# W0 as one transfer on the ScalarE queue, and one filler group fewer before the first transposes

## The chip, the core and the metric

The kernel runs on one core of a Trainium2 chip. The metric is device time in microseconds (us) of one execution. Most numbers below are medians of 3 to 11 executions; a trace is one execution. An execution is called slow when it took over 1.5% longer than the fastest of the same kernel in the same set, and fast otherwise; the ratios below use fast executions alone. Most matmuls of this kernel are printed by the timeline with a tile of 128*32, and the program issues them in sets of four on four such tiles; such a set is called a group. In the traces the four run side by side: in the trace before, a group of 512 columns takes about 0.22 us, less than the 0.38 us (median) that one of its matmuls lasts. The clock record of the trace before has two values, 1.0 and 0.5. I call them full and half clock, and half clock also the time before the first entry, where such a group takes 0.43 us in the trace after.

## The reference, cut to what matters

```python
# x0: 4096 x 416, ws: 6 x 416 x 416, bs: 6 x 416, all bf16
x = x0
for l in range(6):
    x = x0 * (x @ ws[l] + bs[l]) + x
return x
```

The kernel keeps x transposed (features on partitions). The 416 features are three chunks of 128 and a tail of 32. Rows go in four blocks of 1024. A layer of a block is 4.87 us of nearly gapless TensorE work, 24 times.

## The kernel before: the start-up

Only the start-up is touched. Of the first block, three pieces of 256 rows are loaded as they are and transposed on TensorE; its last 256 rows and the other blocks come by transposing transfers. W0, the weights of the first layer, comes in two transfers: its first third (`k == 0`) as the third load of SyncE, the other two thirds as the second load of ScalarE.

```python
# SyncE
sp.dma_start(bsa_sb[1:L + 1, :], bs[:, :]).then_inc(s_bs, 16)
sp.dma_start(xin_sb[:, 0:2, :], x0_v[:, 0:2, :]).then_inc(s_xin[0], 16)   # "x load 0"
sp.dma_start(w_sb[:, 0, 0, :], ws[0, 0:128, :]).then_inc(s_w0, 16)
sp.dma_start(xin_sb[:, 4:6, :], x0_v[:, 4:6, :]).then_inc(s_xin[2], 16)
sp.dma_start_transpose(x0T_sb[:, :, 768:SB], x0[768:SB, 0:DF]).then_inc(s_x0T[0], 16)
# ... cut: W1 to W5 and the other blocks of x
# ScalarE
act.dma_start(xin_sb[:, 2:4, :], x0_v[:, 2:4, :]).then_inc(s_xin[1], 16)  # "x load 1"
act.dma_start(w_sb[:, 0, 1:NC, :], ...).then_inc(s_w[0], 16)
act.dma_start(xtl_sb[:, :, :], x0_v[:, 6:JS, DF:D]).then_inc(s_xtl0, 16)  # "x tail load"
# ... cut
# TensorE
def fill(n):              # matmuls of constants whose result nobody reads
    for i in range(n):
        for q in range(4):
            tile_mm(ps[lane(q), 7, 0:256], const[:, 0:32], const, q, True)
fill(10)
bias_sums()
fill(2)
pe.wait_ge(s_set, 1)
for i, (h, c) in enumerate(IN_ORDER):      # six transposes of x load 1, then six of x load 0
    if c == 0:
        pe.wait_ge(s_xin[h], 16)
    # ... cut: two transposes into PSUM, then s_inT
# layer 0 of block 0
pe.wait_ge(s_w0, 16)
for k in range(NC):
    if k == 1:
        pe.wait_ge(s_w[0], 16)
    if k == 2:
        pe.wait_ge(s_xin[2], 16); pe.wait_ge(s_xtl0, 16)
        tail_inputs(); third_input()
    before_a(k)           # k == 0: waits for three VectorE copies of transposed x
    for m in range(NC):
        # ... cut
        step(m, 0, k)
```

The filler is meant to keep TensorE busy until the loads land. After this part TensorE goes on to the tail matmuls (those that read the 32-feature tail), and from there everything is periodic.

Of the kernel before, what the change touches and what calls it, by code (L numbers as in the profile page):

```python
# [11 lines left out]
def bass_standalone__dcn_v2_cross__recsys_kernel(  # L12
# [8 lines left out]
    NC = 3  # L21
    DF = 128 * NC
# [10 lines left out]
    with ExitStack() as es:  # L33
        block = es.enter_context(nc.Block())

        def sb(name, shape, dt=BF16):
            return es.enter_context(nc.sbuf_tensor(name, shape, dt))

        w_sb = sb("w_sb", [128, L, NC, D])
# [23 lines left out]
        def sem(name):  # L63
            return es.enter_context(nc.semaphore(name))

        s_ones, s_set, s_w0, s_zero = sem("s_ones"), sem("s_set"), sem("s_wk0"), sem("s_zero")
        s_wtp, s_wc = sem("s_wtp"), [sem("s_wc%d" % i) for i in range(2)]
        s_bs, s_cbp, s_cb = sem("s_bs"), sem("s_cbp"), sem("s_cb")
        s_xin = [sem("s_xin%d" % i) for i in range(3)]
# [1 line left out]
        s_w = [sem("s_w%d" % i) for i in range(L)]  # L71
# [15 lines left out]
        def wmain(l):  # L87
            return ws[l, 0:DF, :].rearrange("(k p) n -> p k n", p=128)
# [10 lines left out]
        def lane(g):  # L99
            return slice(32 * g, 32 * g + 32)  # L100
# [4 lines left out]
        def load_wt(eng, g, a, b, done):  # L105
            n0, n1 = ((0, 256), (256, DF))[g % 2]
            eng.dma_start(
                wt_sb[lane(g), a:b, 0:n1 - n0], ws[a:b, DF:D, n0:n1].rearrange("l p n -> p l n")
            ).then_inc(done, 16)

        @block.sync
        def _(sp):
            def load_rows(s):
                sp.dma_start_transpose(
                    x4_sb[:, s - 1:s, :], x0[s * SB:(s + 1) * SB, D - 128:D]
                ).then_inc(s_x4[s - 1], 16)
                sp.dma_start_transpose(
                    x0T_sb[:, :, s * SB:(s + 1) * SB], x0[s * SB:(s + 1) * SB, 0:DF]
                ).then_inc(s_x0T[s], 16)

            sp.dma_start(bsa_sb[1:L + 1, :], bs[:, :]).then_inc(s_bs, 16)  # L121
            sp.dma_start(xin_sb[:, 0:2, :], x0_v[:, 0:2, :]).then_inc(s_xin[0], 16)  # L122
            sp.dma_start(w_sb[:, 0, 0, :], ws[0, 0:128, :]).then_inc(s_w0, 16)
            sp.dma_start(xin_sb[:, 4:6, :], x0_v[:, 4:6, :]).then_inc(s_xin[2], 16)
            sp.dma_start_transpose(x0T_sb[:, :, 768:SB], x0[768:SB, 0:DF]).then_inc(s_x0T[0], 16)
            for l in range(1, L):
                if l > 1:
                    sp.wait_ge(s_ti, (1, 2, 2, 2)[l - 2])
                if l == L - 1:
                    load_rows(1)  # L130
                sp.dma_start(w_sb[:, l, :, :], wmain(l)).then_inc(s_w[l], 16)
                if l == 1:
                    for g in range(4):
                        load_wt(sp, g, 1, L, s_wt[1])
            for s in range(NS - 1):
                n = (s + 1) * L
                sp.wait_ge(s_xa, NC * n)
                sp.wait_ge(s_xb, NC * n)
                for c in range(NC):
                    sp.dma_start_transpose(  # L140
                        o_sb[:, s * JS:(s + 1) * JS, c * 128:(c + 1) * 128], xo_sb[:, s, c, :]
                    ).then_inc(s_oT, 16)
                sp.wait_ge(s_xt, n)
                sp.dma_start_transpose(ot_sb[:, s, :, :], xot_sb[:, s, :]).then_inc(s_ot, 16)
                if s < NS - 2:
                    load_rows(s + 2)
                sp.wait_ge(s_oT, 16 * NC * (s + 1))
                sp.wait_ge(s_otc, s + 1)
                sp.dma_start(
                    out_v[:, s * JS:(s + 1) * JS, :], o_sb[:, s * JS:(s + 1) * JS, :]  # L150
                ).then_inc(s_out, 16)
            j = (NS - 1) * JS
            sp.wait_ge(s_oeA, 2)
            sp.dma_start(out_v[:, j:j + 4, 0:256], o_sb[:, j:j + 4, 0:256]).then_inc(s_out, 16)
            sp.wait_ge(s_oeA, 3)
            sp.wait_ge(s_oet, 1)
            sp.dma_start(out_v[:, j:j + 4, 256:D], o_sb[:, j:j + 4, 256:D]).then_inc(s_out, 16)
            sp.wait_ge(s_oeD, 2)
            sp.wait_ge(s_oet, 1)
            sp.dma_start(out_v[:, j + 6:j + 8, :], o_sb[:, j + 6:j + 8, :]).then_inc(s_out, 16)  # L160
            sp.wait_ge(s_out, 16 * (NS + 3))
# [48 lines left out]
        def _(pe):  # L210
            def tile_mm(dst, lhsT, rhs, q, start):
                return pe.matmul(  # L212
                    dst, lhsT=lhsT, rhs=rhs, start=start, stop=True,
                    skip_group_check=True, tile_position=(0, 32 * q),
                )
# [3 lines left out]
            def fill(n):  # L219
# [4 lines that stand above are left out]
            def tail_inputs():  # L224
                for r in range(2):
                    for g in range(4):
                        for i in range(2):
                            j = 2 * (g ^ i) + r
                            src = xin_sb[:, j, DF:D] if j < 6 else xtl_sb[:, j - 6, :]
                            ins = tile_mm(ps[lane(g), 5, i * G + r * 128:i * G + r * 128 + 128], src, ident[:, :], g, True)  # L230
                ins.then_inc(s_tp, 1)

            def third_input():
                pe.wait_ge(s_inD, 4)
                for c in range(NC):
                    for j in range(2):
                        for q in range(4):
                            f0 = c * 128 + 32 * q
                            ins = tile_mm(
                                ps[lane(q), THIRD[c], j * 128:j * 128 + 128], xin_sb[:, 4 + j, f0:f0 + 32], ident[:, :], q, True  # L240
                            )
                    ins.then_inc(s_inT, 1)

            def bias_sums():
                pe.wait_ge(s_bs, 16)
                pe.wait_ge(s_zero, 2)
                pe.wait_ge(s_set, 2)
                for c in range(NC + 1):
                    for q in range(4):
                        f0 = c * 128 + 32 * q if c < NC else DF  # L250
                        ins = tile_mm(ps[lane(q), 1, c * 8:c * 8 + L], bsa_sb[:, f0:f0 + 32], u_sb[:, :], q, True)
                ins.then_inc(s_cbp, 1)

            fill(10)
            bias_sums()
            fill(2)
            pe.wait_ge(s_set, 1)
            for i, (h, c) in enumerate(IN_ORDER):
                if c == 0:
# [17 lines left out]
            for s in range(NS):  # L277
                for l in range(L):
                    n = s * L + l
# [25 lines left out]
                    def before_a(k):  # L305
                        if n == 0:
                            pe.wait_ge((s_inD, s_inA, s_inD)[k], (3, 2, 4)[k])
                        else:
                            pe.wait_ge(s_xa, NC * (n - 1) + k + 1)
                            if l == 0 and k == 0:  # L310
                                pe.wait_ge(s_x0T[s], 16)

                    if n == 0:
                        pe.wait_ge(s_w0, 16)
                        for k in range(NC):
                            if k == 1:
                                pe.wait_ge(s_w[0], 16)
                            if k == 2:
                                pe.wait_ge(s_xin[2], 16)
                                pe.wait_ge(s_xtl0, 16)  # L320
                                tail_inputs()
                                third_input()
                            before_a(k)
                            for m in range(NC):
                                if k == 0 and m == 1:
                                    pe.wait_ge(s_cb, 1)
                                step(m, 0, k)
                    else:
                        if s == 0:
                            pe.wait_ge(s_w[l], 16)  # L330
                        chunk(0, 0, before_a)
                        chunk(1, 0)
                        chunk(2, 0)
# [140 lines left out]
        @block.scalar  # L474
        def _(act):
            act.dma_start(xin_sb[:, 2:4, :], x0_v[:, 2:4, :]).then_inc(s_xin[1], 16)
            act.dma_start(w_sb[:, 0, 1:NC, :], ws[0, 128:DF, :].rearrange("(k p) n -> p k n", p=128)).then_inc(s_w[0], 16)
            act.dma_start(xtl_sb[:, :, :], x0_v[:, 6:JS, DF:D]).then_inc(s_xtl0, 16)
            for g in (1, 3):
                load_wt(act, g, 0, 1, s_wt[0])  # L480
# [15 lines left out]
            for s in range(NS):  # L496
                for l in range(L):
                    n = s * L + l + 1
# [75 lines left out]
```

## Time and profile before

| | before |
|---|---|
| median, first 3 executions (range) | 131.13 us (130.83 to 131.14) |
| span of the profiled execution | 128.6 us |
| layer 0 starts | 5.46 us |
| tail matmuls start | 8.15 us |

Three lines of the page of the kernel before: TensorE's busy time with its share of the span, then the chain of work that ended last, by engine and by line.

```profile
PE 124.0 (96%) x2440; PEld 62.3 (48%) x2440; DVE 100.1 (78%) x154; ACT 71.4 (56%) x163; POOL 22.5 (18%) x41
PE 92%; DMA 3%; DVE 1%; SPq 1%; issue 0%; DVEq 0%
PE ps L212 82%; PE ps L353 10%; DMA w_sb<-in_ws_dram 3%; DVE xo_sb L461 1%; DVE o_sb L466 0%; SPq L122 0%; SPq L121 0%; DVEq L33 0%; PE ps L369 0%
```

So TensorE is the bound, and the only load in the chain is W0. The chain of the first 9 us, in order of time (start, duration, what; SPq is SyncE's queue):

```profile
0.81 0.39 SPq L121
1.26 0.42 SPq L122
1.73 3.68 DMA w_sb<-in_ws_dram
5.41 0.04 issue
5.46 2.76 PE ps L212 x75
8.22 0.32 PE ps L353
```

In this execution layer 0 starts because the first third of W0 lands at 5.41 us, and from there TensorE is never released by a load again. The timeline of the same kernel (start, duration, engine, line, operation, count, and the idle time before it in brackets) shows the rest of the start-up:

```profile
3.30 0.62 PE L212 MATMUL ps<-const-bfloat16-1.0 128*32 128x256 bf16 x8
3.85 1.46 PE L262 MATMUL ps<-ident,xin_sb 128*128 128x128 bf16 x12
4.28 1.36 DVE L438 COPY x0T_sb<-ps 128x256 bf16<-128x256 bf16 x4 [0.65 <-PE ps L262]
5.46 1.55 PE L212 MATMUL ps<-x0T_sb,w_sb 128*32 128x512 bf16 x24
5.76 0.75 PEld L212 LDWEIGHTS ps<-x0T_sb,w_sb 128*32 128x32 bf16 x16 [0.17 <-issue]
8.15 0.39 PE L353 MATMUL ps<-x0t_sb,wt_sb 32*128 32x512 bf16 x1
```

The twelve transposes run without a break, and the 24 first matmuls of layer 0, six groups of 512 columns, take 1.55 us: about 0.22 us a group after the first. A filler group of only 256 columns takes 0.21 us, so the array then runs at half the rate. The page's PEclk row prints full clock in every slice and does not show this; the clock record in the trace file does: its first entry is full clock, and it begins at 5.66 us. (The half clock before the first entry is not in the mean granted clock of an execution either: this one's mean is 1.000.)

### The profile page before, as it was taken

What the parts mean: (1) busy time and instruction counts of PE and PEld (TensorE: products, weight loads), DVE (VectorE), ACT (ScalarE), POOL (GpSimd) and SP (SyncE); (2) the same over time, 40 slices, a digit from 0 to 9 for tenths busy, and PEclk for the clock granted to TensorE, in tenths of its full rate; (3) what the DMA queues carried; (4) which work ended last, traced back from release to release, by engine and by line L of the source; (5) the groups of instructions that cost most, each with busy time, mean ns of one, the idle gap of its engine ahead of it and who ended that gap; (6) DMA issues with size and microseconds to landing.
All of it is one profiled execution on the core that took longest, in us unless ns stands there. A gap on an engine that the chain in (4) does not pass through costs nothing.

```text
span 128.6 us, 5388 instructions
## 1 busy us (share of the span) xinstructions
PE 124.0 (96%) x2440; PEld 62.3 (48%) x2440; DVE 100.1 (78%) x154; ACT 71.4 (56%) x163; POOL 22.5 (18%) x41
## 2 busy tenths in 40 slices
PE   7999999999999999999999999999999999999980
PEld 5564544545444444444444445445445445445450
DVE  2349779779779779779779779779779779789780
ACT  0637357377737357377736456476745555555670
POOL 7502202202202103102102113012012013022130
PEclk9999999999999999999999999999999999999999
DMA  3974399500009689700009686800009800800026
GB/s 102 293 175 105 90 230 167 148 0 5 3 11 140 128 130 211 255 0 5 5 0 180 117 158 146 270 0 0 5 0 85 190 0 0 270 0 5 3 79 191
DMA packets 32898, 12.54 MB, mean 98 GB/s; under 512 B 25318, under 2 KB 32876, under 8 KB 32876
## 3 DMA queue, kind: packets, MB, share of 16 engines
q1 hardware_dynamic: 31500, 11.48, 43.2%
q10 hardware_dynamic: 1184, 0.67, 1.9%
q8 instruction: 19, 0.31, 1.0%
q0 software_dynamic: 192, 0.06, 0.2%
q14 instruction: 3, 0.02, 0.1%
HBM read 2.90 MB, written 3.41 MB: 49 GB/s over the span
## 4 chain that ended last, share of the span: by engine, by line
PE 92%; DMA 3%; DVE 1%; SPq 1%; issue 0%; DVEq 0%
PE ps L212 82%; PE ps L353 10%; DMA w_sb<-in_ws_dram 3%; DVE xo_sb L461 1%; DVE o_sb L466 0%; SPq L122 0%; SPq L121 0%; DVEq L33 0%; PE ps L369 0%
## 5 line engine op out<-in xcount | busy, mean ns | idle before, releaser
L461 DVE SCALAR_TENSOR_TENSOR xT_sb<-ps,cb_sb,x0T_sb 128x512 bf16<-128x512 f32 x120 | 80.9, 743 | 16.4 <-PE ps L353 16.4
L212 PE MATMUL ps<-xT_sb,w_sb 128*32 128x512 bf16 (+1 forms) x1680 | 89.0, 364 | 0.0
L212 PEld LDWEIGHTS ps<-xT_sb,w_sb 128*32 128x32 bf16 x1680 | 43.1, 97 | 38.6 <-issue 4.2
L488 ACT ACTIVATE xt_sb<-xt_sb 32x256 bf16<-32x256 bf16 x80 | 33.1, 414 | 16.6 <-POOL xt_sb L199 15.9
L508 ACT ACTIVATE t_sb<-ps,cb_sb 64x256 f32<-64x256 f32 x48 | 22.5, 468 | 30.1 <-PE ps L212 29.8
L199 POOL TENSOR_TENSOR xt_sb<-t_sb,x0t_sb 128x256 bf16<-128x256 f32 x20 | 13.4, 672 | 84.1 <-ACT t_sb L508 84.1
L212 PE MATMUL ps<-x0T_sb,w_sb 128*32 128x512 bf16 (+1 forms) x336 | 18.5, 365 | 0.1
L461 DVE SCALAR_TENSOR_TENSOR xo_sb<-ps,cb_sb,x0T_sb 128x512 bf16<-128x512 f32 x23 | 15.6, 744 | 3.7 <-PE ps L353 3.3
L212 PEld LDWEIGHTS ps<-x0T_sb,w_sb 128*32 128x32 bf16 x336 | 8.5, 97 | 7.9 <-issue 1.0
L353 PE MATMUL ps<-xt_sb,wt_sb 32*128 32x512 bf16 x80 | 12.2, 380 | 0.0
L521 ACT ACTIVATE x0t_sb<-x_sb 32x256 bf16<-32x256 bf16 x24 | 9.9, 413 | 0.4
L369 PE MATMUL ps<-xt_sb,wt_sb 32*128 32x512 bf16 x40 | 7.8, 386 | 0.0
L353 PE MATMUL ps<-xt_sb,wc_sb 32*128 32x256 bf16 x80 | 7.7, 268 | 0.0
L353 PEld LDWEIGHTS ps<-xt_sb,wt_sb 32*128 32x128 bf16 x80 | 2.3, 93 | 8.5 <-DVE xT_sb L461 8.5
L353 PEld LDWEIGHTS ps<-xt_sb,wc_sb 32*128 32x128 bf16 x80 | 4.0, 94 | 2.3
L199 POOL TENSOR_TENSOR xot_sb<-t_sb,x0t_sb 128x256 bf16<-128x256 f32 x4 | 2.7, 671 | 12.6 <-ACT t_sb L508 12.6
L212 PE MATMUL ps<-const-bfloat16-1.0 128*32 128x256 bf16 x48 | 2.9, 414 | 0.8 <-PEq L559 0.8
L483 ACT ACT_TABLE_LOAD x1 | 1.3, 1283 | 3.3 <-issue 3.3
L353 PE MATMUL ps<-x0t_sb,wt_sb 32*128 32x512 bf16 x16 | 2.4, 380 | 0.0
L212 PEld LDWEIGHTS ps<-const-bfloat16-1.0 128*32 128x32 bf16 x48 | 1.7, 133 | 1.1 <-issue 0.8
L168 POOL DMA_DIRECT2D wc_sb<-in_ws_dram x4 | 2.2, 550 | 0.0
L443 DVE CAST x0T_sb<-ps 128x256 bf16<-128x256 f32 x2 | 0.8, 420 | 1.8 <-PE ps L212 1.8
(43 smaller groups left out, 28.8 us busy)
## 6 DMA issues: line engine op xcount, KB each, us to landing
out_dram<-o_sb SPq DMA_DIRECT2D x3, 832.0 KB, 4.1
w_sb<-in_ws_dram SPq DMA_DIRECT2D x5, 312.0 KB, 4.3
xin_sb<-in_x_dram SPq DMA_DIRECT2D x2, 208.0 KB, 3.5
out_dram<-o_sb SPq DMA_DIRECT2D x1, 256.0 KB, 2.4
xin_sb<-in_x_dram ACTq DMA_DIRECT2D x1, 208.0 KB, 2.7
w_sb<-in_ws_dram ACTq DMA_DIRECT2D x1, 208.0 KB, 3.4
out_dram<-o_sb SPq DMA_DIRECT2D x1, 208.0 KB, 2.2
out_dram<-o_sb ACTq DMA_DIRECT2D x1, 208.0 KB, 2.7
```

Of the source, the lines that this page charges most:

```text
L168: pool.dma_start(wc_sb[lane(g), a:b, 32 * g:32 * g + 32], ws[a:b, DF:D, DF:D].rearrange("l p n -> p l n")).then_inc(s_wc[i], 16)
L199: pool.tensor_tensor(out=dst, in0=t32_sb[:, n % 2, :], in1=x0t_sb[:, s, 0:G], op=ALU.mult).then_inc(s_xt, 1)
L212: return pe.matmul(dst, lhsT=lhsT, rhs=rhs, start=start, stop=True, skip_group_check=True, tile_position=(0, 32 * q),)
L353: return pe.matmul(dst, lhsT=lhsT, rhs=srct[lane(g), cols], start=l == 0 and start, stop=True, skip_group_check=True, tile_position=(32 * ...
L369: pe.matmul(ps[:, NC * h + 2, :], lhsT=wt_sb[lane(g), l, 0:128], rhs=srct[lane(g), :].rearrange("p (b r) -> p b r", b=2)[:, ::-1, :], star ...
L443: dve.tensor_copy(out=x0T_sb[:, c, 512:768], in_=ps[:, THIRD[c], 0:G]).then_inc(s_inD, 1)
L461: dve.scalar_tensor_tensor(out=dst, in0=ps[:, NC * half + c, :], scalar=cb_sb[:, c, l:l + 1], in1=x0T_sb[:, c, o:o + H], op0=ALU.add, op1= ...
L483: act.activation(out=x0T_sb[:, 1, h * 256:(h + 1) * 256], in_=psT[:, IN_BANKS[h][1], 0:256], func=ACTF.Copy).then_inc(s_inA, 1)
L488: ins = act.activation(out=buf[lane(g), G:2 * G], in_=buf[lane(g ^ 1), 0:G], func=ACTF.Copy)
L508: ins = act.activation(out=t32_sb[HALVES[h], n % 2, :], in_=tail(h), func=ACTF.Identity, bias=cb_sb[HALVES[h], NC, l:l + 1],)
L521: ins = act.activation(out=x0t_sb[lane(g), s + 1, swap * G:(swap + 1) * G], in_=x4_sb[96:128, s, r * G:(r + 1) * G], func=ACTF.Copy,)
```

## The change

The intent: the first layer should not wait for a third load of SyncE when ScalarE's second load brings the rest of the same matrix earlier; and with an earlier start, less filler is needed.

```diff
-            sp.dma_start(w_sb[:, 0, 0, :], ws[0, 0:128, :]).then_inc(s_w0, 16)
...
             fill(10)
             bias_sums()
-            fill(2)
+            fill(1)
...
-                        pe.wait_ge(s_w0, 16)
+                        pe.wait_ge(s_w[0], 16)
                         for k in range(NC):
-                            if k == 1:
-                                pe.wait_ge(s_w[0], 16)
...
-            act.dma_start(w_sb[:, 0, 1:NC, :], ...).then_inc(s_w[0], 16)
+            act.dma_start(w_sb[:, 0, :, :], wmain(0)).then_inc(s_w[0], 16)
```

Cut: the semaphore `s_w0` is no longer made.

More of the change, by code (lines that the diff above doesn't have):

```diff
@@ L64, in sem @@
             return es.enter_context(nc.semaphore(name))
-        s_ones, s_set, s_w0, s_zero = sem("s_ones"), sem("s_set"), sem("s_wk0"), sem("s_zero")
+        s_ones, s_set, s_zero = sem("s_ones"), sem("s_set"), sem("s_zero")
         s_wtp, s_wc = sem("s_wtp"), [sem("s_wc%d" % i) for i in range(2)]
@@ L476, in _ @@
             act.dma_start(xin_sb[:, 2:4, :], x0_v[:, 2:4, :]).then_inc(s_xin[1], 16)
-            act.dma_start(w_sb[:, 0, 1:NC, :], ws[0, 128:DF, :].rearrange("(k p) n -> p k n", p=128)).then_inc(s_w[0], 16)
+            act.dma_start(w_sb[:, 0, :, :], wmain(0)).then_inc(s_w[0], 16)
             act.dma_start(xtl_sb[:, :, :], x0_v[:, 6:JS, DF:D]).then_inc(s_xtl0, 16)
```

## The prediction

> **What bounds the kernel.** TensorE. The page gives PE 124.0 us of a 128.6 us span (96%), and the chain of work that ended last is 92% PE, 3% "DMA w_sb". Every later layer takes 4.87 us, which the change doesn't touch. Only the first 8.7 us can move.
>
> **The start-up before (timeline, chain, transfers).** Filler, bias sums, 8 fillers from 3.30 to 3.92 us, 12 transposes from 3.85, layer 0 from 5.46. The chain there reads: SyncE issues 0.81 and 1.26, then the first third of W0 from its issue at 1.73 for 3.68 us, so it lands at 5.41. The other two thirds (ScalarE queue, issued 1.27, 3.4 us) land at 4.65. Layer 0 also needs the third VectorE copy of the transposed x, which ends at 5.21: a limit only 0.2 us behind.
>
> **What the change does.**
> - The first third of W0 moves from SyncE's third place to ScalarE's second: one transfer of 312 KB, where there were 208 KB. The 208 KB had sent their packets by about 4.25 us; the extra 104 KB are 128 packets of 832 bytes, 0.32 us at the observed 40 packets per 100 ns, twice that if shared with SyncE's next load. My estimate for the landing of all of W0 is 5.15 us (4.95 to 5.45). [...]
> - SyncE drops one issue (0.45 us): the third x load (lands 6.35) and the transposed x load (7.92) come up to 0.5 us earlier. Neither ends a wait now. The x tail load on ScalarE gets later, from 5.84 to about 6.2, still in time.
> - One filler group (4 matmuls, 0.21 us a group) goes. The first transposes can start at about 3.64, as x of the first two blocks landed at 3.49. The second half waits for a load that landed at 4.23; its transposes began at 4.46. So the third copy ends near 5.04.
>
> **On the path.** Layer 0 should start at about 5.22, 0.24 us earlier. That isn't kept whole: before 5.66 us the clock is half. The trace's clock record gives full clock only from 5.66 us on; a filler group of 256 columns takes 0.21 us, as does a group of 512 columns later. [...] Work done before 5.66 counts half, so the gain is about 0.12 us.  The wait at 8.05 is for copies of the third x block, which move with TensorE itself.
>
> **Predicted: 131.0 us**, range 130.5 to 131.5; faster by over 2%: 0.01, within 2%: 0.98, slower by over 2%: 0.01.
>
> **What would show it.** W0 as one transfer landing between 4.95 and 5.45 us; first transpose near 3.64; first layer-0 matmul near 5.2; full clock from about 5.66; first tail matmuls about 0.1 us before 8.15; 4.87 us per layer unchanged.
>
> **What would make it wrong.** (a) W0 lands after 5.41: then no gain, or a loss of some tenths, again halved by the cold clock. [...] (c) The later tail load or tail weights end a wait at 6.6 or 8.0.

It came to this: layer 0 starts at 5.22 us instead of 5.46, 0.24 us earlier; work before 5.66 us counts half, so 0.12 us are left, and 131.13 us (the median before) less 0.12 us is 131.0 us. The landing of W0, 5.15 us, was an estimate from the trace before: it lies between 4.65 + 0.32 = 4.97 us and 4.65 + 0.64 = 5.29 us, the second if another load shares the time. That loads share it the trace does show: from 3.5 to 4.0 us one of the two hardware queues moved 171 packets and the other 50, and from 3.2 to 3.5 us 29 and 101, at 341 and 355 GB/s in all.

## The result, and the profile after

| | before | after |
|---|---|---|
| median of 6 executions (range) | 131.05 us (130.78 to 131.22) | 130.74 us (130.29 to 132.34) |
| ratio of the fast executions | 1 | 0.9969, 95% interval 0.9946 to 0.9992 |
| profiled execution | 130.45 us, fast | 132.34 us, slow |

A ratio here is the mean time of one kernel's fast runs over the mean of the other's fast runs of the same rounds, so it is not quite the ratio of the medians. The ratio leaves out the slow execution; with it the means are 130.94 us after and 131.01 us before. One of the six executions after is 1.1 us longer than any other of the two kernels in this table (132.34 against 131.22), and it is the one that was profiled. I use its trace to see what a slow execution is, not for the size of the gain.

The chain of the kernel after (line numbers have moved by 1 to 3):

```profile
0.81 0.39 SPq L121
1.27 3.33 DMA xin_sb<-in_x_dram
4.61 0.05 issue
4.65 0.82 PE ps L261 x6
5.47 0.05 issue
5.52 4.51 PE ps L211 x76
10.04 0.32 PE ps L350
```

W0 has left the chain: as one transfer it landed at 5.11 us. In its place stands x load 0, which landed at 4.61 us here against 4.23 us in the trace before, with the same issue and nothing in its own queue changed ahead of it. And the matmuls that took 2.76 us from the start of layer 0 to the tail matmuls now take 4.51 us. The timeline of the kernel after says why:

```profile
3.31 0.40 PE L211 MATMUL ps<-const-bfloat16-1.0 128*32 128x256 bf16 x4
3.73 1.74 PE L261 MATMUL ps<-ident,xin_sb 128*128 128x128 bf16 x12
4.65 0.55 PEld L261 LDWEIGHTS ps<-ident,xin_sb 128*128 128x128 bf16 x6 [0.39 <-DMA xin_sb<-in_x_dram]
5.52 2.75 PE L211 MATMUL ps<-x0T_sb,w_sb 128*32 128x512 bf16 x24
5.90 0.18 PEld L211 LDWEIGHTS ps<-x0T_sb,w_sb 128*32 128x32 bf16 x4 [0.25 <-issue]
6.33 0.18 PEld L211 LDWEIGHTS ps<-x0T_sb,w_sb 128*32 128x32 bf16 x4 [0.25 <-issue]
6.75 0.18 PEld L211 LDWEIGHTS ps<-x0T_sb,w_sb 128*32 128x32 bf16 x4 [0.25 <-issue]
9.97 0.38 PE L350 MATMUL ps<-x0t_sb,wt_sb 32*128 32x512 bf16 x1
```

The weight loads come 0.42 to 0.43 us apart: a group of 512 columns takes twice its time of before. The clock record agrees: full clock from 9.31 us, not from 5.66 us. The transposes are now broken in two by the wait for x load 0. After the start-up nothing differs: from the start of the tail matmuls to the end of the span it is 128.6 - 8.15 = 120.5 us before and 130.5 - 9.97 = 120.5 us after.

So two questions are open. Does the change itself make the clock late, or can that happen to the kernel before too? And is the gain of 0.3 us of the fast executions a gain of the change?

### The profile page after: what moved, and what is told of

Same layout as the page of the kernel before. It is cut to its first block, busy times and chain, and to the rows that moved or that the text cites. A ratio compares the mean times of both kernels' runs of the same rounds, so it can differ in the third digit from the quotient of the medians.

```text
span 130.5 us, 5378 instructions
## 1 busy us (share of the span) xinstructions
PE 125.8 (96%) x2436; PEld 62.9 (48%) x2436; DVE 100.3 (77%) x154; ACT 71.5 (55%) x163; POOL 22.6 (17%) x41
## 3 DMA queue, kind: packets, MB, share of 16 engines
HBM read 2.90 MB, written 3.41 MB: 48 GB/s over the span
## 4 chain that ended last, share of the span: by engine, by line
PE 93%; DMA 3%; DVE 1%; SPq 0%; issue 0%; DVEq 0%
PE ps L211 82%; PE ps L350 10%; DMA xin_sb<-in_x_dram 3%; PE ps L261 1%; DVE xo_sb L458 1%; DVE o_sb L463 0%; SPq L121 0%; DVEq L33 0%; PE ps L366 0%
## 5 line engine op out<-in xcount | busy, mean ns | idle before, releaser
L211 PE MATMUL ps<-x0T_sb,w_sb 128*32 128x512 bf16 (+1 forms) x336 | 19.8, 383 | 0.0
L489 ACT ACTIVATE x0t_sb<-ps 128x512 bf16<-128x512 f32 x1 | 0.6, 597 | 3.1 <-PE ps L211 3.1
```

The lines of the kernel that those rows point to most:

```text
L211: return pe.matmul(dst, lhsT=lhsT, rhs=rhs, start=start, stop=True, skip_group_check=True, tile_position=(0, 32 * q),)
L489: act.activation(out=x0t_sb[:, 0, :], in_=ps[:, 5, :], func=ACTF.Copy).then_inc(s_te, 1)
```

## The experiments

All runs gave correct results.

### Each part alone, and the change again

Theory: the two parts together start layer 0 earlier (W0 by the merge, the copies by the dropped filler). Rivals: one part alone gives it; or it is luck of the clock and of the loads.

`after_again` is the changed kernel without an edit. Its trace was hoped to be of a fast execution, but it is of a slow one too (132.50 us).

> The changed kernel itself, to have its trace in the fast state and more executions of it. Theory E (earlier start): first layer-0 matmul near 5.25 us, W0 landed by 5.2, full TensorE clock by about 5.9 us at the latest, median 130.7. Theory L ([...] the gain of 0.3 us is only a difference in when the full clock comes): the layer-0 start is as in the kernel before, 5.45, and the times lie around 131.0. On the slow execution (132.34): [...] at least one of these executions is again above 132; if it was chance, none.

`merge_only` keeps both filler groups:

```diff
-            fill(1)
+            fill(2)
```

> W0 as one transfer, with both filler groups kept. Theory W (the transfer alone gives the gain, as only W0 was waited for): 130.75, layer-0 start limited by the VectorE copies at 5.3. Theory C (both parts are needed, the copies are the next limit 0.2 us behind): about 130.9, half of the gain, since the third copy still ends near 5.2. No execution above 132 if the dropped filler group is what lets the clock come late.

`filler_only` is the kernel before with the one line

```diff
-            fill(2)
+            fill(1)
```

> One filler group fewer, W0 still in two transfers. Theories W and C both: first transposes near 3.65 us, third copy ending near 5.05, but layer 0 still starts at 5.45 when the first third of W0 lands at 5.41: 131.05, no gain. Theory F (the filler group itself is on the path): 130.75. If the dropped group is what lets the clock come late, an execution above 132 can show here as well.

`merge_fill0` is the changed kernel with no filler there at all:

```diff
-            fill(1)
```

> The changed kernel with no filler between the bias sums and the first transposes. The x load of the first transposes lands at 3.5 to 3.6 us, so they can't start earlier than with one group (3.7): no gain in the fast executions, 130.7. [...] there are more executions above 132 than in the changed kernel (at least 2 of 5); if the slow state is chance alone, as many.

| run | median (range), us | ratio of fast runs (95%) |
|---|---|---|
| before, same rounds, 11 executions | 131.12 (130.48 to 132.42) | 1 |
| after_again | 131.10 (130.28 to 133.20) | 0.9956 (0.9896 to 1.0016) |
| merge_only | 130.54 (130.19 to 131.18) | 0.9941 (0.9891 to 0.9992) |
| filler_only | 130.42 (129.96 to 132.68) | 0.992 (0.9867 to 0.9973) |
| merge_fill0 | 131.03 (130.59 to 131.92) | 0.9976 (0.9919 to 1.0033) |

The intervals are wide because the kernel before had three executions above 132 us among its eleven (132.17, 132.32, 132.42), which the 1.5% rule still counts as fast. The same rule leaves out 132.68 us of filler_only and 132.50 and 133.20 us of after_again, so the ratios of this set flatter the other kernels. With every execution above 132 us left out on both sides, the means are 130.34 us for filler_only, 130.63 for merge_only and 131.07 for merge_fill0, against 130.97 for the kernel before.

So the first question is answered in part: **the kernel before has such long executions as well**. They left no trace, and that their clock was late is my estimate. Their spans (130.4 to 130.6 us) and mean granted clock (0.993) are those of the trace after (130.5 us, 0.994). There the full clock lasts 119.47 us and is followed by 1.7 us of half clock at the end. A mean of 0.993 also makes about 1.8 us of half clock at the end; 119.47 us counted back from there give a full clock at 9.1 to 9.3 us. The theory that only the dropped filler makes the long executions is refuted.

Two expectations failed here. after_again had layer 0 at 5.55 us (5.25 expected) and full clock at 9.65 us (5.9 at the latest), and two executions above 132 us, as the reading that blames the dropped filler had it. But merge_fill0, with less filler still, had none above 132 us, where that reading expected at least two of five. The number of filler groups alone does not decide.

The second is not. No theory expected that filler_only would do best, as it leaves the late W0 transfer alone. Its trace shows how it could: there the first third of W0 landed at 5.02 us, not at 5.41. The chain of filler_only:

```profile
3.71 0.73 PE ps L262 x6
4.43 0.02 issue
4.46 0.59 DVE x0T_sb L438 x2
5.04 0.14 issue
5.18 2.69 PE ps L212 x76
```

W0 is not in this chain; the copies are. And merge_only, whose W0 comes as one transfer, waits for it until 5.33 us:

```profile
1.27 4.06 DMA w_sb<-in_ws_dram
5.33 0.05 issue
5.38 2.69 PE ps L211 x76
```

What limits layer 0 changes from execution to execution, with either form of the W0 load.

### The clock taken out of the question (two tries, both weak)

To see the order of the loads without the clock, I let VectorE run 44 small memsets ("ticks"), TensorE run one filler group at each, and all loads wait for the last tick. The later filler was doubled in number, as groups take half the time at full clock (0.22 us against 0.43 us for one of 512 columns).

```diff
+            for i in range(TICKS):          # VectorE, TICKS = 44
+                dve.memset(tick_sb[:, i, :], 0.0).then_inc(s_tick, 1)
...
+            sp.wait_ge(s_tick, TICKS)       # before the first load; ScalarE and GpSimd likewise
...
-            fill(10)
+            for i in range(TICKS):
+                pe.wait_ge(s_tick, i + 1)
+                fill(1)
+            fill(20)
             bias_sums()
-            fill(2)
+            fill(4)                         # 2 where the change drops a group
```

> The kernel before with the clock taken out of the question: 44 ticks of a VectorE memset (about 0.2 us each) delay every load, and TensorE runs one filler group at each tick, so that the full clock is reached before the first load is issued; the later fillers are doubled in number, as each takes half the time. Theory P (the spread of 128.2 to 131.5 us of span comes from when the full clock arrives): full clock before the first load, executions within 0.3 us of each other, none of them 1.5 us longer; about 140 us. Rival D (the spread comes from late loads): the spread stays over 1 us. Seen from the first load's issue, layer 0 starts 4.6 us later, when the first third of W0 lands.

> Warm clock, one filler group's time fewer, W0 in two transfers. The loads end the waits here, so theory W (the W0 transfer is the only limit) expects no difference from warm_before (within 0.1 us); theory F (the filler is on the path) expects 0.2 us less.

> Warm clock, W0 as one transfer, filler as before. Theory W: layer 0 starts 0.2 to 0.3 us earlier than in warm_before, and at full clock all of it is kept: 0.2 to 0.3 us less. Rival N (the order of the bytes gives nothing; the 0.3 us measured was the clock's phase): within 0.1 us of warm_before. Rival T: the start is earlier but the later x tail load ends a new wait at the transposes of the tail, and the gain is given back there.

> Warm clock, both parts of the change. Theory W: as warm_merge_only, 0.2 to 0.3 us less than warm_before. Rival N: within 0.1 us of warm_before. Rival T: W0 lands earlier, but the tail transposes wait for the x tail load.

| run (4 executions each) | median (range), us |
|---|---|
| warm_before | 139.05 (138.66 to 139.24) |
| warm_filler_only | 139.00 (138.82 to 140.00) |
| warm_merge_only | 139.83 (139.22 to 140.37) |
| warm_after | 139.66 (138.50 to 140.17) |

This was a flawed experiment. A tick took 0.11 us (the last came 4.7 us after the first; the expectation below says 0.13), less than a filler group at half clock (0.21 us), so TensorE was behind and still running filler 5.0 to 5.5 us after the first load was issued. In all four traces layer 0 began after filler, transposes and copies, not after a load, so the four times say little about the order of the loads. Nor do they show that the merge costs time, though warm_merge_only took 0.8 us more than warm_before: of the 0.56 us between their two traces, 0.52 us lie after the last matmul (4.50 against 3.99 us; 3.45 us in the kernel before). Theory P's spread of 0.3 us failed too: the four had 0.58 to 1.67 us. warm_filler_only shows how late a small load can be; its chain has

```profile
8.08 7.50 DMA xtl_sb<-in_x_dram
```

The x tail load, 16 KB, took 7.50 us, where in the other traces it takes 3.8 to 5.9 us (4.0 in the kernel before). That execution took 140.00 us, the other three 138.82 to 139.08 us. So by this one trace a late load alone can cost about a microsecond, and part of the spread may be that.

The mended pair has ticks of 0.17 us on average (44 in 7.67 us), and TensorE was done with the filler 3.1 to 3.3 us after the first load was issued.

> The warm experiment again, mended: in the first try a tick took 0.13 us, so TensorE was still working off its filler 4.9 us after the first load was issued and the loads ended no wait. Now a tick is about 0.22 us, as long as a filler group at half clock. Seen from the first load's issue the transposes start by 3.1 us, the copies end by 4.2 us and layer 0 of the kernel before starts when the first third of W0 lands, 4.2 to 5.4 us. Theory P: no execution is 1.5 us longer than the others; what spread is left (up to 1 us) is that of the loads.

> As warm2_before, with the change. Theory W (all of W0 lands earlier, at 4.2 to 4.5 us from the first issue in all merged traces so far): layer 0 starts at about 4.4 us, and the kernel takes 0.3 to 0.6 us less than warm2_before. Rival T: the start is as early, but the x tail load, which lands at 5.0 to 5.7 us, ends a new wait and takes back part: 0 to 0.3 us less. Rival N: same within 0.1 us, layer 0 starting at the same time.

warm2_before took 141.06 us (140.75 to 142.89) and warm2_after 141.19 us (140.91 to 142.91), 6 executions each. The chains:

```profile
10.01 4.44 DMA xin_sb<-in_x_dram
14.49 0.30 PE ps L268 x2
14.81 0.30 DVE x0T_sb L446
15.25 2.68 PE ps L215 x76
```

for warm2_before, and for warm2_after

```profile
10.01 5.14 DMA w_sb<-in_ws_dram
15.24 2.75 PE ps L214 x76
```

Layer 0 starts 5.70 us (before) and 5.69 us (after) after the first load is issued. W0 as one transfer landed at 5.60 us, the first third alone at 5.53 us. This is what the rival expected for which the order of the bytes gives nothing. But the loads fell differently here than in the plain kernels: x load 0 landed 4.9 us after the first issue in both, where 3.3 to 3.8 is usual, and I don't know why. One of the six executions of warm2_before (142.89 us) and two of warm2_after (142.39 and 142.91 us) are over a microsecond longer than the rest, with a mean granted clock of 0.981, 0.989 and 0.979. So the spread did not go away as theory P had it. But the clock was not out of the question either. The mean counts the half clock after the first full clock, and in the first and the last of the three that comes to 5.4 and 5.9 us, against at most 2.5 us in the nine shorter executions (0.991 of 139.1 us). These are estimates from the means; the executions left no trace, and why they are long stays open.

### The gaps filled

The stretches of full clock in the traces' clock records last 122.88 us (before), 119.47 us (after), and in longer traces of the experiment before 129.71 and 133.12 us: 36, 35, 38 and 39 times 3.413 us. So I divided the time before the full clock into windows of that length, counted back from where the record says full clock begins. That such a window has to do with the clock is my assumption. From ten traces I worked out how much of each window the array had columns to process, counting 1.2 columns per ns (256 columns in 0.213 us, as the filler shows) and counting matmuls that run side by side once. The table has been completed with the later runs; left out are windows with a share of 0.58 or less, none of which had the full clock at its end; the last windows of merge_fill0, after, after_again and filler_only_again, of 0.94 to 1.00, which all did; and the traces of the experiment before, whose windows of 0.83 to 1.00 all did:

| trace | window, us | share | full clock at its end? |
|---|---|---|---|
| filler_only | 0.79 to 4.20 | 0.85 | yes |
| merge_only | 1.17 to 4.58 | 0.84 | yes |
| plugged | 3.08 to 6.50 | 0.80 | yes |
| before | 2.24 to 5.66 | 0.77 | yes |
| filler_only_again | 3.57 to 6.98 | 0.74 | no |
| filler_only_again | 0.16 to 3.57 | 0.70 | no |
| merge_fill0 | 0.49 to 3.90 | 0.70 | no |
| after | 2.48 to 5.90 | 0.69 | no |
| after_again | 2.82 to 6.24 | 0.68 | no |
| plugged | -0.33 to 3.08 | 0.62 | no |

The share orders the two groups without an exception, with the border between 0.74 and 0.77. A recount that places the columns 0.19 us later in time moves single shares by up to 0.06 and keeps the two groups apart. Without the twelve transposes the order breaks: about 0.41 in the window of before, which had the full clock at its end, and 0.69 in the first of filler_only_again, which had not. So if a share decides, transposes count in it. If it decides, keeping TensorE busy in its two waits should bring the clock at the end of the first window that fits:

```diff
+            def plug(n, bank):
+                for i in range(n):
+                    for q in range(4):
+                        tile_mm(ps[lane(q), bank, 0:128], const[:, 0:32], const[:, 0:128], q, True)
...
                 if c == 0:
+                    if h == 0:
+                        plug(2, 6)          # before the wait for x load 0
                     pe.wait_ge(s_xin[h], 16)
...
+            plug(2, 2)                      # after the last transpose, before layer 0
```

> The changed kernel with TensorE kept busy in its two waits: two filler groups of 128 columns (0.21 us at half clock) before the second six transposes, and two before layer 0. In ten traces so far the full clock came after each window of 3.41 us in which TensorE's array streamed columns for 0.77 or more of the time, and not after windows of 0.70 or less. Theory A (that share decides): with the gaps plugged every window that starts after 0.85 us holds more than 0.77, so the full clock comes by 7.1 us at the latest, and no execution is above 131.5; median 130.5. Rival B (late clocks are the loads' doing or chance): about one execution in five is above 132 as before, and the added fillers cost up to 0.2 us: median 131.0.

plugged: 130.91 us (130.65 to 134.67); before in the same rounds 131.05 us (130.68 to 132.85); ratio 0.9979 (0.994 to 1.0018). Five of its six executions lie within 0.32 us of each other. The sixth is 134.67, more than any other, so theory A's "none above 131.5" failed. That execution left no trace. By my estimate, a full clock 3.41 us later costs half of that at half clock, 1.7 us, and one 6.83 us later 3.4 us, which would come near (134.3 us); but by theory A those windows, full of layer 0, should have passed. Rival B (131.0 us, about one execution in five above 132) fits these six times better than theory A (130.5 us). The trace of the profiled one does fit A, with full clock at 6.50 us. It shows TensorE without a gap, and the price of it:

```profile
4.39 0.40 PE L211 MATMUL ps<-const-bfloat16-1.0 128*32 128x128 bf16 x8
4.73 0.82 PE L268 MATMUL ps<-ident,xin_sb 128*128 128x128 bf16 x6
5.48 0.40 PE L211 MATMUL ps<-const-bfloat16-1.0 128*32 128x128 bf16 x8
5.67 1.88 PE L211 MATMUL ps<-x0T_sb,w_sb 128*32 128x512 bf16 x24
```

x load 0 had landed at 4.13 us, so the second six transposes waited for filler, and layer 0 started at 5.67 us. What the plug may give in the clock (full at 6.50 us, against 9.31 in the trace after) it takes back in part in the start (5.67 us, against 5.52). It beats neither kernel clearly.

### The filler part once more

filler_only had the best median and an interval that excludes 1. I repeated the same file.

> The kernel with one filler group fewer and W0 in two transfers once more; its five fast executions averaged 130.34 us against 130.96 of 30 fast executions of the kernel before. Theory F (the dropped group is worth something by itself: when the first third of W0 lands by 5.05 us, as in that trace, the copies are the limit, and they come 0.2 us earlier): fast executions again average 130.3 to 130.6. Rival L (the clock and the loads fell well in five executions): 130.8 to 131.0. [...]

It took 132.05 us (131.06 to 132.89); before in the same rounds 130.69 us (130.20 to 132.19, 11 executions); ratio 1.0072 (1.0021 to 1.0122). **The same kernel was 0.8% faster in one set and 0.7% slower in the next, and both intervals exclude 1.** The 1.5% rule sharpened both: it kept three long executions of the kernel before in the first set and left out one (132.19 us) in the second. With all above 132 us left out, the mean is 0.5% lower in the first set and 0.4% higher in the second (131.22 us, of two executions, against 130.65), so the sign still changes. The first set ran on another chip (11) than the second (4); that the chip makes the difference was not tested. The trace of the second set shows the opposite luck:

```profile
1.73 3.92 DMA w_sb<-in_ws_dram
5.65 0.04 issue
5.70 4.96 PE ps L212 x73
10.66 0.32 PE ps L353
```

The first third of W0 landed at 5.65 us (5.02 in the first set), TensorE stood idle before layer 0, the window from 3.57 to 6.98 us came to a share of 0.74, and full clock came at 10.40 us. Theory F (130.3 to 130.6 us again) failed. Rival L (luck) is nearer as to the cause, as far as one trace tells, but its numbers, 130.8 to 131.0, were missed by a microsecond.

### All traces of the plain kernels in one table

Times in us from the span's start; "W0" is the landing of the part that layer 0 first needs.

| trace | x load 0 | W0 | third copy | layer 0 | full clock | tail matmuls | span | span minus tail |
|---|---|---|---|---|---|---|---|---|
| before | 4.23 | 5.41 | 5.21 | 5.46 | 5.66 | 8.15 | 128.6 | 120.5 |
| filler_only | 4.37 | 5.02 | 5.03 | 5.18 | 4.20 | 7.80 | 128.3 | 120.5 |
| filler_only_again | 4.40 | 5.65 | 5.17 | 5.70 | 10.40 | 10.59 | 131.1 | 120.5 |
| merge_only | 4.58 | 5.33 | 5.24 | 5.38 | 4.58 | 8.00 | 128.5 | 120.5 |
| after | 4.61 | 5.11 | 5.38 | 5.52 | 9.31 | 9.97 | 130.5 | 120.5 |
| after_again | 4.63 | 5.04 | 5.40 | 5.55 | 9.65 | 10.15 | 130.6 | 120.4 |
| merge_fill0 | 4.18 | 5.04 | 5.03 | 5.18 | 7.32 | 8.83 | 129.3 | 120.5 |
| plugged | 4.13 | 4.99 | 5.45 | 5.67 | 6.50 | 8.68 | 129.1 | 120.4 |

The last column is constant to 0.1 us: in these traces the whole difference between 128.3 and 131.1 us of span is made before the tail matmuls. There the start of layer 0 moves by 0.5 us and the full clock by 6 us. merge_fill0 and filler_only start layer 0 at the same 5.18 us, and still their tail matmuls are 1.03 us apart, because the full clock came at 7.32 and at 4.20 us.

## Why the prediction was right, and where it was not

**The time.** 131.0 us was predicted with 130.5 to 131.5; 130.74 us was measured, and "within 2%" holds. That says little for the mechanism: the kernel before, at 131.05 us, lies in the same range. The size of the gain is less sure than that sounds. The prediction had 0.12 us; the rounds gave 0.31 us, and a second set of the same kernel 131.10 against 131.12 us; with all executions above 132 us left out on both sides, the means of that set are 130.82 us (4 executions) against 130.97 us (8). A gain of a few tenths for the change is neither shown nor excluded: executions of the kernel before alone ran from 130.20 to 132.85 us over the 46 that were timed, and its medians from 130.69 to 131.12 us in the five sets.

**W0 as one transfer lands between 4.95 and 5.45 us.** Right: 5.11 and 5.04 us in the two traces of the change, 4.99 to 5.33 in the other merged ones.

**The first transpose near 3.64 us.** Right: 3.73 and 3.64 us.

**"So the third copy ends near 5.04" and layer 0 starts "at about 5.22".** Wrong in both traces of the change: 5.38 and 5.40, and 5.52 and 5.55 us. Both are of slow executions; no fast execution of the change left a trace, so where layer 0 starts in those is not known (the nearest fast traces, merge_only and merge_fill0, have 5.38 and 5.18 us). The step took the landing of x load 0 of one trace, 4.23 us, as a property of the kernel. It landed at 4.61 and 4.63 us. In eight traces it lies between 4.13 and 4.63. Whether the larger W0 transfer beside it makes it later is not settled: with W0 in two transfers it landed at 4.23 to 4.40 us in three traces, with W0 as one at 4.13 to 4.63 in five. The same holds for the step before it: that W0 lands at 5.41 and is the limit was one draw. With W0 in two transfers, the first third landed at 5.41, 5.02 and 5.65 us in three traces.

**"Work done before 5.66 counts half."** The mechanism was right: groups of 512 columns 0.43 us apart before the full clock, 0.22 us after it. The date was wrong. The full clock came between 4.20 and 10.40 us. A later full clock was named among the risks. What was measured: the slow execution took 132.34 us against a mean of 130.65 us of the other five, 1.7 us or 1.3% more, and its full clock came at 9.31 us. The prediction gave such a delay too little weight. Two things could have caused it; neither is shown to. A longer idle gap is in the trace (the transposes broken in two); less filler cannot be needed for it, as the kernel before has long executions too: 6 of 46 above 132 us, against 3 of 12 of the change. These counts don't tell the two apart. Counted over all kernels, one group dropped has 8 of 24 (the change and filler_only), both kept 6 of 52 (before and merge_only), none kept 0 of 6 (merge_fill0). I grouped them after the fact, so this is a hint at most.

I used 5.66 us, the date in one trace, as a constant. It is none: the full clock begins at another time in each of the eight traces of the table.

**Does the change make the slow state more likely?** There is an argument for it, not a proof. In the window from 2.24 to 5.66 us the array's share was 0.77 in the trace before and 0.69 in the trace after, over the same stretch. The difference is 0.08 x 3.41 = 0.27 us, and the dropped filler group is 0.21 us of it: when x load 0 is late, the group is not replaced by earlier work but by waiting. If there is a border between 0.74 and 0.77, before passes and after doesn't. That the share decides rests on the order of ten windows; I did not vary it alone, the trace after is one of a slow execution, and the outlier of plugged is unexplained.

## What to carry to other kernels

When a start-up lies under half a clock and a handful of loads, one trace shows one draw: take several before calling a transfer the limit, and repeat a result of half a per cent in another set, even if its interval excludes 1. Price a change of the start-up in two currencies, when the work can start and when the full clock comes (0.5 us and 6 us apart between the traces here); filler ahead of landed data costs time (in plugged the second six transposes began at 4.73 us, though their load had landed at 4.13 us). The rest of the kernel tells where to look: here the time after the start-up was constant to 0.1 us, so all that was found lies in its first 10 us.
